# A fused MLP on one core: the first token chunk loaded and turned in two halves, with a new order of the first matmuls

## The chip, the cores and the metric

The kernel runs on one core of one Trainium2 chip. The metric is the device time of one execution in microseconds. Before the change the median of five runs is 93.78 us (93.72 to 94.08).

## The reference

The kernel computes a two-layer perceptron with a tanh-approximated GELU on 2048 tokens, 448 features and 1792 hidden units, all in bf16:

```
B, S, D, F = 1, 2048, 448, 1792
h = jnp.einsum("bsd,df->bsf", x, w1) + b1
h = jax.nn.gelu(h, approximate=True)
return jnp.einsum("bsf,fd->bsd", h, w2) + b2
```

## The kernel before

**Tiling.** The tokens are worked in four chunks of 512 (SC = 512, HC = 256). A chunk runs layer 1 completely, and then layer 2. Layer 1 puts hidden units on the 128 partitions and 512 tokens on the free axis: 14 F-tiles of 128 hidden units, taken as 7 pairs. The 448 features are contracted as three full slices of 128 (k = 0, 1, 2) and a remainder of 64 (k = 3). Layer 2 puts tokens on the partitions and contracts the 14 F-tiles.

**Two half-arrays.** Every contraction of 128 rows is split into two of 64 rows, one on each half of the TensorE array, so matmuls come in twos that run side by side on two PSUM banks. Of an F-tile pair, part "a" gives tile 0 the lower rows and tile 1 the upper ones, and part "b" the other way round. Part "a" has the slices k = 0 to 2; part "b" has these and the remainder. For the remainder the rows of w1 are in w1r: loaded on the upper 64 partitions, and copied for the odd tiles to the lower ones by VectorE (L399, event w1rU). In this text a "step" is one such couple of matmuls for one k; L0.a(0,256) means part a of pair 0 on the first 256 tokens, three half-wide steps.

**PSUM.** There are four units of two banks; units go round: pair 0 has u0, pair 1 u1, pair 2 u2, pair 3 u3, pair 4 u0 again. A pair may start when the two GELU activations that read its unit's former content are done. ScalarE does one activation of 128x512 for each F-tile (L269), with the bias b1.

**The start.** Chunks 1 to 3 of x are turned by DMA transposes. Chunk 0 is loaded as it stands (xn, L153) with four consecutive tokens on each partition, and TensorE turns it by 64-row transposes against an identity (L344): for every half h of 256 tokens and every slice k, one block of four transposes, and four for the remainder rows out of xr, which VectorE has collected from xn (L362). Copies out of PSUM into xT follow, on VectorE and ScalarE (L357 for the slices, L384 for the remainder). Until x is there, TensorE runs 7 dependence-free matmuls of 512 columns and one of 256 (warm, L192).

**Queues.** Loads come from two hardware queues. The queue of SyncE (SPq, DMA queue q1) issues x, then waits until ScalarE has loaded its table (an activation on a constant), and then issues w1r's first part, w1's third part (F-tiles 4 to 7), w1r's second part, w1's fourth part (tiles 8 to 13), w2 in two parts, b2, and the transposes. The queue of ScalarE (ACTq, DMA queue q10) issues w1's first two parts: ("w1", 0) with F-tiles 0 and 1, ("w1", 1) with tiles 2 and 3. b1 comes over GpSimd's queue, and VectorE turns it (four 32x32 transposes, L181, and a cast, L183) after the copy of w1r's first part and before that of its second.

**The order of the work** is written out by hand: each engine executes its list in order, and each instruction waits for the events that it names. On TensorE at the start the list is: warm; the first half's blocks; L0.a(0,256); the last block and the remainder's; L1.a(0,256); L0.a(256,512); L1.a(256,512); L0.b; L1.b; L2.a; and from there L3.a, L2.b, L4.a, L3.b and so on, all 512 wide. The two blocks of the second half for k = 0 and 1 go with the first half's, ahead of L0.a.

Of the kernel before, what the change touches and what calls it, by code (L numbers as in the profile page):

```python
# [7 lines left out]
BF16 = mybir.dt.bfloat16  # L8
# [65 lines left out]
def bass_standalone__dense_activation_gelu__prompt_kernel(  # L74
# [8 lines left out]
    B, S, D = x.shape  # L83
    F = w1.shape[1]
    P = 128
    H = P // 2
    SC = 512
    HC = SC // 2
    assert B == 1 and S % SC == 0 and F == 14 * P and D == 3 * P + H
    x2, out2 = x[0], out[0]  # L90
    NSC, NST, STC, NFT = S // SC, S // P, SC // P, F // P
    NPAIR = NFT // 2
    KT = 3
    D3 = KT * P
    DH = D // 2
    NWARM = 7

    with ExitStack() as es:
        sb = lambda name, shape, dt: es.enter_context(nc.sbuf_tensor(name, shape, dt))
        xn = sb("xn", [P, STC, D], BF16)  # L100
        xr = sb("xr", [P, STC // 2, P], BF16)
        ident = sb("ident", [P, P], BF16)
        xT = sb("xT", [P, KT + 1, S], BF16)
# [10 lines left out]
        out_sb = sb("out_sb", [P, NST, D], BF16)  # L114
        unit = [es.enter_context(nc.psum_tensor(f"u{i}", [P, 2, SC], FP32)) for i in range(4)]

        pr = Program(nc, es)
# [10 lines left out]
        def load_w1(i, engine="sync"):  # L128
            c0, c1 = W1CUTS[i] * P, W1CUTS[i + 1] * P
            pr.dma(engine, lambda e: e.dma_start(  # L130
                w1_sb[:, :, c0:c1], w1[0:D3, c0:c1].rearrange("(k p) f -> p k f", p=P)), ("w1", i))
# [3 lines left out]
        def load_w1r(i, engine="sync"):  # L135
            cs = slice(RCUTS[i] * P, RCUTS[i + 1] * P)
            pr.dma(engine, lambda e: e.dma_start(w1r[H:P, cs], w1[D3:D, cs]), ("w1r", i))

        def load_w2(a, b):
            pr.dma("sync", lambda e: e.dma_start(  # L140
                w2_sb[:, a:b, :], w2[a * P:b * P, :].rearrange("(f p) d -> p f d", p=P)), ("w2", a))
# [6 lines left out]
                xT[:, slot, s0:s1], x2[s0:s1, d0:d0 + P], transpose=True), event, after)  # L148


        x0v = x2[0:SC, :].rearrange("(p t) d -> p t d", t=STC)
        o0v = out2[0:SC, :].rearrange("(p t) d -> p t d", t=STC)
        pr.dma("sync", lambda e: e.dma_start(xn[:, :, :], x0v), "x")  # L153
        pr.barrier("sync", ["table"])
        load_w1r(0)
        load_w1(2)
        load_w1r(1)
        load_w1(3)
        load_w2(0, 7)
# [2 lines left out]
        for c in range(1, NSC):  # L162
            for slot in range(KT + 1):
# [5 lines left out]
            out=ident[:, :], in_=ident[:, :], compare_op=ALU.not_equal, fill=1.0,  # L169
# [4 lines left out]
               after=["b1z"])  # L174
        pr.op("scalar", lambda e: e.activation(junk[:, :], one, ACT.Gelu_apprx_tanh), event="table")  # L175
        load_w1(0, "scalar")
        load_w1(1, "scalar")

        def turn_b1():
            for q in range(4):  # L180
                pr.op("vector", lambda e, q=q: e.transpose(  # L181
                    b1t[32 * q:32 * q + 32, :], b1n[:, 32 * q:32 * q + 32]), after=["b1n"], event=("b1t", q))
            pr.op("vector", lambda e: e.tensor_copy(b1_f[:, :], b1t[:, 0:NFT]),  # L183
                  after=[("b1t", q) for q in range(4)], event="b1")
# [5 lines left out]
        def warm(n, cols=SC):  # L190
            for _ in range(n):
                pr.op("tensor", lambda e: e.matmul(unit[0][:, 0, 0:cols], lhsT=ones_w, rhs=ones_m[:, 0:cols],  # L192
                                                   start=True, stop=True))
# [3 lines left out]
        busy = {}  # L197
# [24 lines left out]
        class Layer1:  # L222
# [33 lines left out]
                for k in range(KT):  # L256
                    self.step("a", k, t0, t1)

            def b(self, t0=0, t1=SC):
                for k in range(KT + 1):  # L260
                    self.step("b", k, t0, t1)
                if t1 == SC:
                    self.act()

            def act(self):
                c, u = self.c, self.u
# [5 lines left out]
                    busy[(u, lo)] = ("g", c, ft)  # L272

        def store(j, after):
            pr.dma("sync", lambda e: e.dma_start(o0v[:, j, :] if j < STC else out2[j * P:(j + 1) * P, :], out_sb[:, j, :]), "out", after=after)

        class Layer2:

# [58 lines left out]
        def spot(u, i, rows=slice(0, P)):  # L337

            return unit[u][rows, :, i * H:(i + 1) * H].bitcast(BF16).rearrange("p b (t s) -> p b t s", t=2)

        def turn(o, i, event, after):

            for half, rows in enumerate(HALVES):
                pr.op("tensor", lambda e, half=half, rows=rows: e.transpose(o(half), i(rows), ident[rows, rows]),  # L344
                      after=["ident"] + after, event=event if half else None)

        def turn_block(h, k, u, i, wait=()):
            for t in (0, 1):
                turn(lambda half, t=t: spot(u, i)[:, half, t, :], lambda rows, t=t: xn[rows, 2 * h + t, k * P:(k + 1) * P],
                     ("xt", h, k) if t else None, ["x"] + list(wait))  # L350

        def drain_blocks(engine, h, ks, u, wait=None):
            n = len(ks)
            o = xT[:, ks[0]:ks[0] + n, h * HC:(h + 1) * HC].rearrange("p k (t b s) -> p k b t s", b=2, t=2)
            f = unit[u][:, :, 0:n * H].bitcast(BF16).rearrange("p b (k t s) -> p k b t s", k=n, t=2)
            for i in range(n):
                pr.op(engine, lambda e, i=i: (e.copy if engine == "scalar" else e.tensor_copy)(o[:, i], f[:, i]),  # L357
                      after=[wait or ("xt", h, ks[-1])], event=("xT0", h, ks[i]))
            busy[(u, 0)] = ("xT0", h, ks[-1])

        def turn_first():
            pr.op("vector", lambda e: e.tensor_copy(  # L362
                xr[:, :, :].rearrange("p q (two h) -> p q two h", two=2),
                xn[:, :, D3:D].rearrange("p (q two) h -> p q two h", two=2)), after=["x"], event="xr_in")
            for k, engine in enumerate(("vector", "scalar", "vector")):
                turn_block(0, k, k, 0)
                drain_blocks(engine, 0, (k,), k)
            turn_block(1, 0, 3, 0)
            turn_block(1, 1, 3, 1)
            drain_blocks("scalar", 1, (0, 1), 3)  # L370

        def turn_rest():


            turn_block(1, 2, 2, 0, [("xT0", 0, 2)])
            for q in range(STC // 2):
                turn(lambda half, q=q: spot(2, 1)[:, half, q, :], lambda rows, q=q: xr[rows, q, :], ("xr", q), ["xr_in"])
            drain_blocks("vector", 1, (2,), 2, ("xr", 1))
            for src, engine in enumerate(("vector", "scalar")):
                i = spot(2, 1, HALVES[src])  # L380
                for dst in (src, 1 - src):
                    o = xT[HALVES[dst], KT, 0:SC].rearrange("p (q two b s) -> p b q two s", q=2, two=2, b=2)[:, :, :, src, :]
                    pr.op(engine, lambda e, o=o, i=i, engine=engine:
                          e.copy(o, i) if engine == "scalar" else e.tensor_copy(o, i),  # L384
                          after=[("xr", 1), ("xT0", 1, 2)], event=("xR0", dst, src))
            busy[(2, 1)] = ("xR0", 1, 0)
            busy[(2, 2)] = ("xR0", 0, 1)

        warm(NWARM)
        warm(1, HC)  # L390
        turn_first()
        L = [Layer1(0, j) for j in range(NPAIR)]
        L[0].a(0, HC)
        turn_rest()

        for i in (0, 1):
            odd = lambda rows, i=i: w1r[rows, RCUTS[i] * P:RCUTS[i + 1] * P].rearrange(
# [2 lines left out]
                  after=[("w1r", i)], event=("w1rU", i))  # L400
            if i == 0:
                turn_b1()
        L[1].a(0, HC)
        L[0].a(HC, SC)
        L[1].a(HC, SC)
        L[0].b()
        L[1].b()
        L[2].a()
        for j in range(3, NPAIR):
            L[j].a()  # L410
            L[j - 1].b()
        L[-1].b()

        for c in range(NSC):
# [7 lines left out]
            else:  # L422

                pr.op("vector", lambda e: e.tensor_copy(b2_z[H:H + 1, :], b2_bc[H:H + 1, :]),  # L424
                      after=["b2", "b2z0"], event="b2z")
# [3 lines left out]
            p = Layer2(c, (0, 1))  # L429
            if c + 1 < NSC:  # L430
                q = Layer2(c, (2, 3))
# [5 lines left out]
            else:  # L437
                q, r = Layer2(c, (2,)), Layer2(c, (3,), True)
# [37 lines left out]
```

## Time and profile before

| | us |
|---|---|
| median of five runs | 93.78 |
| the profiled execution, whole | 93.8 |
| its span, first to last instruction | 92.5 |
| TensorE busy in the span | 89.2 |
| ScalarE busy | 38.4 |
| VectorE busy | 13.5 |
| first matmul of the warm-up | 0.78 |
| first transpose of x | 4.17 |
| first matmul of layer 1 | 4.93 |
| second group of layer 1 (pair 1) | 5.56 |

A busy time is the sum over the time in which the engine had at least one instruction in work. The difference of 1.3 us between the execution and its span lies ahead of the first and behind the last instruction. Times of single instructions below are counted from the start of the span. In a line of the timeline the columns are: start, length, engine, source line, operation, what it writes and reads, and how many instructions were merged; in brackets, idle time of that engine ahead of it and what ended it.

### The profile page before, as it was taken

To read this page: it belongs to the slowest core of one execution; us is meant where nothing else is said; L and a number is where in the kernel's file an instruction comes from. 1 tells how busy PE (TensorE), PEld (TensorE's weight loads), DVE (VectorE), ACT (ScalarE), POOL (GpSimd) and SP (SyncE) were. 2 spreads that over 40 slices of the span, in tenths; PEclk is the share of its full clock that TensorE was granted. 3 is DMA by queue.
4 is the path that set the end of the run, shared out by engine and by line. 5 is a ranking of instruction groups with operands and counts; after the bars stand their busy time and mean duration, and the time that the engine had idled before them with its cause. 6 is when DMAs were issued, how large, how long until landed. Compare 5 with 4: busy or idle time off the path is not lost.

```text
span 92.5 us, 2086 instructions
## 1 busy us (share of the span) xinstructions
PE 89.2 (96%) x945; PEld 45.8 (50%) x945; DVE 13.5 (15%) x34; ACT 38.4 (42%) x64; POOL 1.7 (2%) x8
## 2 busy tenths in 40 slices
PE   6989999999999999999999999999999999999990
PEld 2374444555544444555554444555554444475890
DVE  0165001100441000000432000000333000000421
ACT  6064978600005788700003787900002888900001
POOL 6000000000000000000000000000000000000000
PEclk9999999999999999999999999999999999999999
DMA  2999999549247000000033000000022000000022
GB/s 48 330 290 328 380 323 135 118 99 109 56 96 216 4 7 0 0 0 0 0 105 101 0 4 0 7 0 0 0 99 99 7 0 0 0 0 7 27 72 99
DMA packets 12744, 7.32 MB, mean 79 GB/s; under 512 B 6976, under 2 KB 12544, under 8 KB 12736
## 3 DMA queue, kind: packets, MB, share of 16 engines
q1 hardware_dynamic: 11904, 6.80, 29.6%
q10 hardware_dynamic: 800, 0.39, 1.4%
q8 instruction: 7, 0.11, 0.5%
q14 instruction: 1, 0.01, 0.0%
q0 software_dynamic: 32, 0.00, 0.0%
HBM read 3.79 MB, written 1.84 MB: 61 GB/s over the span
## 4 chain that ended last, share of the span: by engine, by line
PE 96%; DVE 1%; issue 0%
PE u L217 92%; PE u L192 4%; PE u L344 0%; DVE out_sb L326 0%; DVE xT L357 0%
## 5 line engine op out<-in xcount | busy, mean ns | idle before, releaser
L269 ACT ACTIVATE g<-u,b_f 128x512 bf16<-128x512 f32 x56 | 34.9, 686 | 39.4 <-PE u L217 38.0
L217 PE MATMUL u<-w_sb,g 64*128 64x448 bf16 (+1 forms) x504 | 43.2, 328 | 0.0
L217 PE MATMUL u<-xT,w_sb 64*128 64x512 bf16 (+1 forms) x348 | 41.0, 369 | 0.2 <-DVE xT L357 0.2
L217 PEld LDWEIGHTS u<-w_sb,g 64*128 64x128 bf16 x504 | 24.5, 94 | 18.4
L217 PEld LDWEIGHTS u<-xT,w_sb 64*128 64x128 bf16 x348 | 16.8, 94 | 19.4 <-DMA w_sb<-in_w_dram 0.3
L312 DVE TENSOR_TENSOR out_sb<-u,b_bc 128x448 bf16<-128x448 f32 x14 | 8.1, 620 | 60.7 <-PE u L217 60.7
L217 PE MATMUL u<-xT,w1r 64*128 64x512 bf16 x56 | 10.6, 376 | 0.0
L217 PEld LDWEIGHTS u<-xT,w1r 64*128 64x128 bf16 x56 | 2.7, 94 | 3.3
L329 ACT CAST out_sb<-u 128x224 bf16<-128x224 f32 x1 | 0.3, 346 | 9.2 <-PE u L217 9.2
L192 PE MATMUL u<-const-bfloat16-1.0 128*128 128x512 bf16 (+1 forms) x8 | 3.4, 601 | 0.8 <-PEq L461 0.8
L192 PEld LDWEIGHTS u<-const-bfloat16-1.0 128*128 128x128 bf16 x8 | 1.0, 139 | 2.4 <-issue 2.4
L357 ACT COPY xT<-u 128x256 bf16<-128x256 bf16 x3 | 0.9, 380 | 2.3 <-PE u L344 2.3
L175 ACT ACT_TABLE_LOAD x1 | 1.3, 1283 | 0.7 <-PEq L461 0.7
L424 DVE COPY b_z<-b_bc 1x448 bf16<-1x448 bf16 x1 | 0.3, 267 | 6.8 <-DMA b_bc<-in_b_dram 6.8
L187 DVE COPY xT<-xT 64x512 bf16<-64x512 bf16 x3 | 0.9, 289 | 2.2 <-DMA xT<-in_x_dram 2.1
L344 PEld LDWEIGHTS u<-ident,xn 64*128 64x128 bf16 x24 | 0.7, 102 | 0.7 <-issue 0.7
L384 ACT COPY xT<-u 64x256 bf16<-64x256 bf16 x2 | 0.7, 368 | 0.5 <-DVE xT L357 0.5
L357 DVE COPY xT<-u 128x256 bf16<-128x256 bf16 x3 | 0.8, 287 | 0.8 <-PE u L344 0.8
L320 DVE TENSOR_TENSOR out_sb<-u,b_bc 128x448 bf16<-128x448 f32 x1 | 0.6, 625 | 1.7 <-PE u L217 1.7
L181 DVE STREAM_TRANSPOSE b1t<-b1n 32x32 bf16<-32x32 bf16 x4 | 0.8, 202 | 0.1
L344 PE MATMUL u<-ident,xn 64*128 64x64 bf16 x24 | 0.8, 199 | 0.0
L362 DVE COPY xr<-xn 128x256 bf16<-128x256 bf16 x1 | 0.2, 226 | 3.1 <-DMA xn<-in_x_dram 3.1
(18 smaller groups left out, 4.8 us busy)
## 6 DMA issues: line engine op xcount, KB each, us to landing
out_dram<-out_sb SPq DMA_DIRECT2D x16, 112.0 KB, 1.7
w_sb<-in_w_dram SPq DMA_DIRECT2D x2, 784.0 KB, 8.0
w_sb<-in_w_dram SPq DMA_DIRECT2D x1, 576.0 KB, 5.7
xn<-in_x_dram SPq DMA_DIRECT2D x1, 448.0 KB, 3.3
w_sb<-in_w_dram ACTq DMA_DIRECT2D x2, 192.0 KB, 4.1
w_sb<-in_w_dram SPq DMA_DIRECT2D x1, 384.0 KB, 4.6
xT<-in_x_dram SPq DMA_TRANSPOSE x12, 3.5
w1r<-in_w_dram SPq DMA_DIRECT2D x1, 160.0 KB, 4.4
```

The lines of the kernel that those rows point to most:

```text
L175: pr.op("scalar", lambda e: e.activation(junk[:, :], one, ACT.Gelu_apprx_tanh), event="table")
L181: pr.op("vector", lambda e, q=q: e.transpose(b1t[32 * q:32 * q + 32, :], b1n[:, 32 * q:32 * q + 32]), after=["b1n"], event=("b1t", q))
L187: pr.op("vector", lambda e: e.tensor_copy(xT[0:H, KT, s0:s1], xT[H:P, KT, s0:s1]), after=after, event=event)
L192: pr.op("tensor", lambda e: e.matmul(unit[0][:, 0, 0:cols], lhsT=ones_w, rhs=ones_m[:, 0:cols], start=True, stop=True))
L217: o = pr.op("tensor", lambda e: e.matmul(unit[u][:, lo, cols], lhsT=lhsT, rhs=rhs, start=start, stop=stop, skip_group_check=skip), after=a ...
L269: pr.op("scalar", lambda e, lo=lo, ft=ft: e.activation(g[:, ft, c * SC:(c + 1) * SC], unit[u][:, lo, :], ACT.Gelu_apprx_tanh, bias=b1_f[:, ...
L312: pr.op("vector", lambda e, lo=lo, j=j: e.tensor_tensor(out=out_sb[:, j, :], in0=unit[u][:, lo, 0:D], in1=b2_bc[:, :], op=ALU.add), after= ...
L320: pr.op("vector", lambda e: e.tensor_tensor(out=out_sb[:, j, :].rearrange("p (two h) -> p two h", two=2), in0=unit[u][:, :, 0:DH], in1=b2_ ...
L329: pr.op("scalar", lambda e: e.copy(out_sb[:, j, DH:D], unit[u][:, 1, 0:DH]), after=[y[1]], event=("o", j, 1))
L344: pr.op("tensor", lambda e, half=half, rows=rows: e.transpose(o(half), i(rows), ident[rows, rows]), after=["ident"] + after, event=event i ...
L357: pr.op(engine, lambda e, i=i: (e.copy if engine == "scalar" else e.tensor_copy)(o[:, i], f[:, i]), after=[wait or ("xt", h, ks[-1])], eve ...
L384: e.copy(o, i) if engine == "scalar" else e.tensor_copy(o, i),
```

## The change

x of chunk 0 is loaded by two DMAs of 256 tokens each, with two consecutive tokens on a partition. The first is issued on SyncE's queue, the second on ScalarE's behind w1's first part; w1's second part goes over to SyncE's queue, behind the first half of x and ahead of the wait for the table. w1's third part now comes ahead of w1r's first. There is one full warm-up matmul fewer. The first half of x is turned alone (turn_0), and L0.a, L1.a and the slices of L0.b run on it; then the second half is turned (turn_1: blocks k = 0, 2, 1 and the remainder), and the rest of pairs 0 and 1 follows in half-wide steps. The remainder steps of pairs 0 and 1 (b_last), with their activations, come after L2.a. All three copies of the second half wait for transposes of turn_1; before, two of them followed on the first half's blocks. Where xn's rows lie in the output changes with the load, so the stores of chunk 0 are indexed by halves.

```diff
-    NWARM = 7
+    NWARM = 6
...
-        x0v = x2[0:SC, :].rearrange("(p t) d -> p t d", t=STC)
-        o0v = out2[0:SC, :].rearrange("(p t) d -> p t d", t=STC)
-        pr.dma("sync", lambda e: e.dma_start(xn[:, :, :], x0v), "x")
+        def load_x(h, engine):
+            pr.dma(engine, lambda e: e.dma_start(
+                xn[:, 2 * h:2 * h + 2, :], x2[h * HC:(h + 1) * HC, :].rearrange("(p t) d -> p t d", t=2)), ("x", h))
+
+        o0v = [out2[h * HC:(h + 1) * HC, :].rearrange("(p t) d -> p t d", t=2) for h in (0, 1)]
+        load_x(0, "sync")
+        load_w1(1)
         pr.barrier("sync", ["table"])
+        load_w1(2)
         load_w1r(0)
-        load_w1(2)
         load_w1r(1)
         load_w1(3)
...
         load_w1(0, "scalar")
-        load_w1(1, "scalar")
+        load_x(1, "scalar")
...
-            def b(self, t0=0, t1=SC):
-                for k in range(KT + 1):
+            def b_main(self, t0=0, t1=SC):
+                for k in range(KT):
                     self.step("b", k, t0, t1)
-                if t1 == SC:
-                    self.act()
+
+            def b_last(self):
+                self.step("b", KT)
+                self.act()
...
+        def drain_block(engine, h, k, u, i, after):
+            o = xT[:, k, h * HC:(h + 1) * HC].rearrange("p (t b s) -> p b t s", b=2, t=2)
+            f = spot(u, i)
+            pr.op(engine, lambda e: (e.copy if engine == "scalar" else e.tensor_copy)(o, f),
+                  after=after, event=("xT0", h, k))
+            busy[(u, int(engine == "scalar"))] = ("xT0", h, k)
+
+        def turn_0():
+            for k, engine in enumerate(("vector", "scalar", "vector")):
+                turn_block(0, k, k, 0)
+                drain_block(engine, 0, k, k, 0, [("xt", 0, k)])
+
+        def turn_1():
             pr.op("vector", lambda e: e.tensor_copy(
                 xr[:, :, :].rearrange("p q (two h) -> p q two h", two=2),
-                xn[:, :, D3:D].rearrange("p (q two) h -> p q two h", two=2)), after=["x"], event="xr_in")
-            for k, engine in enumerate(("vector", "scalar", "vector")):
-                turn_block(0, k, k, 0)
-                drain_blocks(engine, 0, (k,), k)
+                xn[:, :, D3:D].rearrange("p (q two) h -> p q two h", two=2)), after=[("x", 0), ("x", 1)], event="xr_in")
             turn_block(1, 0, 3, 0)
-            turn_block(1, 1, 3, 1)
-            drain_blocks("scalar", 1, (0, 1), 3)
-        def turn_rest():
-            turn_block(1, 2, 2, 0, [("xT0", 0, 2)])
+            turn_block(1, 2, 3, 1)
+            turn_block(1, 1, 2, 0, [("xT0", 0, 2)])
             for q in range(STC // 2):
                 turn(lambda half, q=q: spot(2, 1)[:, half, q, :], lambda rows, q=q: xr[rows, q, :], ("xr", q), ["xr_in"])
-            drain_blocks("vector", 1, (2,), 2, ("xr", 1))
+            drain_block("vector", 1, 0, 3, 0, [("xt", 1, 2)])
+            drain_block("scalar", 1, 1, 2, 0, [("xr", 1)])
+            drain_block("vector", 1, 2, 3, 1, [("xt", 1, 2)])
...
-        turn_first()
+        turn_0()
         L = [Layer1(0, j) for j in range(NPAIR)]
         L[0].a(0, HC)
-        turn_rest()
+        L[1].a(0, HC)
+        L[0].b_main(0, HC)
+        turn_1()
...
-        L[1].a(0, HC)
-        L[0].a(HC, SC)
-        L[1].a(HC, SC)
-        L[0].b()
-        L[1].b()
+        L[1].b_main(0, HC)
+        for j in (0, 1):
+            L[j].b_main(HC, SC)
+        for j in (0, 1):
+            L[j].a(HC, SC)
         L[2].a()
+        for j in (0, 1):
+            L[j].b_last()
```

More of the change, by code (lines that the diff above doesn't have):

```diff
@@ L257, in a, with b @@
                     self.step("a", k, t0, t1)
-            def b(self, t0=0, t1=SC):
-                for k in range(KT + 1):
+            def b_main(self, t0=0, t1=SC):
+                for k in range(KT):
                     self.step("b", k, t0, t1)
-                if t1 == SC:
-                    self.act()
+            def b_last(self):
+                self.step("b", KT)
+                self.act()
+            def b(self):
+                self.b_main()
+                self.b_last()
             def act(self):
@@ L274, in store @@
         def store(j, after):
-            pr.dma("sync", lambda e: e.dma_start(o0v[:, j, :] if j < STC else out2[j * P:(j + 1) * P, :], out_sb[:, j, :]), "out", after=after)
+            pr.dma("sync", lambda e: e.dma_start(o0v[j // 2][:, j % 2, :] if j < STC else out2[j * P:(j + 1) * P, :], out_sb[:, j, :]), "out", after=after)
         class Layer2:
@@ L349, in turn_block @@
                 turn(lambda half, t=t: spot(u, i)[:, half, t, :], lambda rows, t=t: xn[rows, 2 * h + t, k * P:(k + 1) * P],
[L350 to L359, printed above, removed]
@@ L361, in turn_first @@
-        def turn_first():
+                     ("xt", h, k) if t else None, [("x", h)] + list(wait))
+        def drain_block(engine, h, k, u, i, after):
[8 more added lines that the diff above has]
+                drain_block(engine, 0, k, k, 0, [("xt", 0, k)])
@@ L384, in turn_rest @@
                           e.copy(o, i) if engine == "scalar" else e.tensor_copy(o, i),
-                          after=[("xr", 1), ("xT0", 1, 2)], event=("xR0", dst, src))
+                          after=[("xr", 1), ("xT0", 1, 1)], event=("xR0", dst, src))
             busy[(2, 1)] = ("xR0", 1, 0)
```

## The prediction

> **What bounds the kernel now.** I began with the page: its first line and its chain of work by engine.
>
> ```profile
> span 92.5 us, 2086 instructions
> ...
> PE 96%; DVE 1%; issue 0%
> ```
>
> TensorE carries the whole chain. Only idle or slow TensorE time can be won, so I took the chain next, piece by piece (start, length, what, how many).
>
> ```profile
> 0.78 3.36 PE u L192 x8
> 4.14 0.02 issue
> 4.17 0.30 PE u L344 x4
> 4.47 0.02 issue
> 4.49 0.30 DVE xT L357
> 4.79 0.14 issue
> 4.93 0.50 PE u L217 x6
> 5.43 0.12 PE u L344 x8
> 5.55 0.01 issue
> 5.56 84.75 PE u L217 x903
> 90.31 0.38 DVE out_sb L326
> ```
>
> From 5.56 to 90.31 matmuls stand back to back; an edit that takes none of them away moves the end only by moving that dense stretch. Up to 5.56 the chain is warm-up, transposes, one copy, and L0.a(0,256). What released L1.a at 5.56? It needs w1's second part. The answer on w1's DMAs of ScalarE's queue:
>
> ```profile
> L130 ACTq DMA_DIRECT2D w_sb<-in_w_dram x2: 446/478/511, 0.8 to 1.3; - x2
> ...
> DMA to landing us min/median/max: 3.9/4.1/4.2
> ```
>
> Issued at 0.80 and 1.28 (timeline), they land at 0.80 + 3.9 = 4.7 and 1.28 + 4.2 = 5.5. The load of x lands at 0.75 + 3.3 = 4.05. So a landing, not arithmetic, opens the dense stretch. Then the order in which the queues were served: the DMA answer for 1.7 to 3.2 us, and for 3.65 to 4.3.
>
> ```profile
> q1 hardware_dynamic: 113, 0.40, 88.3%
> ```
>
> ```profile
> q10 hardware_dynamic: 455, 0.22, 115.4%
> ```
>
> First x alone (q1), then both parts of w1 alone (q10), although x and w1's first part were issued within 0.05 us. Last, VectorE's timeline, because "remainder rows late" touches what hangs on it, and the line of the waits that shows it binding:
>
> ```profile
> 6.57 0.22 DVE L399 COPY w1r<-w1r 64x256 bf16<-64x256 bf16 x1
> 6.82 0.90 DVE L181 STREAM_TRANSPOSE b1t<-b1n 32x32 bf16<-32x32 bf16 x4
> 7.86 0.17 DVE L183 CAST b_f<-b1t 128x14 f32<-128x14 bf16 x1
> ```
>
> ```profile
> ACT g L269 <- DVE b_f L183: 1.4, 1, 1.4
> ```
>
> The first activation (8.13) waits for the bias, which waits for the copy of w1r: 8.13 - 6.57 = 1.56 us from that copy's start to the activation.
>
> **What the Trainium skill says.** "DMA: Bandwidth & Descriptors", section "Issuing engines are not separate DMA queues": loads from several queues run on the same 16 DMA engines, so a second queue brings no bandwidth. The trace agrees (the two windows above). The same page, "Queues, rings and completion order": an engine round-robins between queues by packets. Here it served whole loads in turn; I saw no finer mixing. "TensorE: Matmul & The Clock Gate", Part 1: TensorE runs at half clock until a window of about 3.4 us was busy; Part 4 of it says that transposes don't count as busy. The trace agrees on the first: warm-up matmuls of 512 columns start every 0.43 us, later couples of 512 every 0.216 (remainder couples at 7.20 and 8.06 with three others between). Of the first half's transposes 8 start from 4.17 to 4.33 and 12 in the next 0.17 us, so the clock rose near 4.33, 3.55 us after the first matmul. On the second no run here says anything.
>
> **The change part by part.**
>
> *First half of x.* x is 0.46 MB; q1 moved 0.40 MB in 1.5 us at 88%, so 0.30 MB/us, and half of x is 0.75 us less ahead of everything behind it. It lands at about 4.05 - 0.75 = 3.3.
>
> *Warm-up.* One matmul less is 0.43 us: the half-wide last one starts at 3.72 - 0.43 = 3.29 and holds the array 0.21 us, to about 3.51. The first transpose goes from 4.17 to 3.54; x's first half is there, so the warm-up sets this.
>
> *First copies.* Transpose to copy 0.32 (4.17 to 4.49), copy 0.30, copy to matmul 0.14; cold transposes add 0.03: L0.a at 3.54 + 0.79 = 4.33, before 4.93. w1's first part lands at 4.7 - 0.75 = 3.95, hidden.
>
> *Work ahead of the second half.* A half-wide step is 0.109 us (9 steps from 5.56 to 6.55). L0.a ends at 4.66. w1's second part, now third in the line, lands at 5.5 - 0.75 = 4.75; its own issue at about 1.15 on SyncE's queue sits in time in which that queue waited for the table. L1.a starts at about 4.79, and six steps (0.65) end at 5.44.
>
> *Second half of x.* It is the last of the same 0.85 MB that landed by 5.5 before. x landed about 0.4 us after its last packets (by 3.65), w1's second part 0.7 after its own (by 4.8): bounds 5.2 and 5.5. I take 5.25, since its descriptors are x's kind. VectorE's xr copy (0.23) ends at about 5.5.
>
> *Turning it.* 16 transposes at some 15 ns, 5.44 to 5.68; the last four start behind the xr copy. Before, two of the second half's blocks and their copies went under the wait for w1; now all of them are on the path, and what covers their copies is L1.b_main(0,256), 0.33 us, to 6.00. VectorE's first copy starts 0.25 after its transposes (5.36 to 5.61 before), 5.79, ends 6.08: first step of L0.b_main(256,512) at 6.13. ScalarE's copy waits for the last transpose (5.66 + 0.23), takes 0.38, ends 6.27: second step at 6.33. VectorE's other copy ends about 6.29, in time. So 0.23 us of stall. From 6.33, 11 half-wide steps take 1.20: L2.a could start at 7.53. Before, L2.a started at 8.28 with two remainder steps (0.43) done that now come later; like for like 7.85. Gain 0.32 us. Twelve full steps in twenty-four half-wide ones cost 24 x 0.109 - 12 x 0.216, under 0.03 us.
>
> *w1's third part* landed at 2.87 + 4.6 = 7.5; with w1r's 64 KB behind it, 0.2 us sooner, 7.3: hidden, with 0.2 to spare. ScalarE's remainder copies (0.76 from 6.27) free u2 at about 7.05, hidden.
>
> *w1r late.* Its first part now lands where both ended before, between 7.0 and 7.5; I take 7.2. Behind that wait on VectorE stand the turn of b1 and so all activations: the first at 7.2 + 0.02 + 1.56 = 8.78. The two of pair 0 end 1.27 later (the pair lengths of 1.26 and 1.27 in ScalarE's timeline), 10.05, and L4.a, which needs u0, could start at 10.10. TensorE reaches L4.a at 7.53 + 0.65 + 0.43 + 0.65 + 0.86 = 10.12 (before, 10.43). So there is no stall, by 0.02 us; later pairs have 1.51 us on TensorE against 1.27 on ScalarE, so it isn't repeated. If w1r lands at 7.5 it is 0.28 us.
>
> *Stores* of chunk 0 move the same rows of 896 bytes: nothing, hidden under layer 1 of the next chunk.
>
> Sum: a gain of 0.32 (the half-wide steps are in it). The span goes from 92.5 to 92.2; the profiled execution, 93.8 with 1.3 outside its span, is that of the median 93.78: about 93.46.
>
> **The rivals.**
>
> *A, as worked out:* 93.46, by itself 93.3 to 93.55 (second half of x at 5.2 to 5.35). Chance 0.54.
>
> *B, the bias wait takes the gain:* w1r lands at 7.5, L4.a waits until 10.4, and all of the earlier start is idle there: 93.46 + 0.28 = 93.74. For it: a straggling landing of w1's third part at 7.5, whose place w1r inherits. Against: its load is small. 0.13.
>
> *C, the second half of x lands no earlier than w1's second part did (5.5), or the two queues' loads mix and w1's first part lands late:* start of the dense part gains 0.1: 93.65 to 93.75. 0.11.
>
> *D, slower, the clock:* the warm-up ends at 3.51 and TensorE then has only transposes and a pause until 4.33. If that window no longer counts as busy, the clock rises one window later (3.4 us). Cold work costs half its time, up to 1.7 us, less some 0.3 of stalls that it fills: 93.46 + 1.4 = 94.9. It turns faster into slower once more than (0.32 + 0.28) x 2, 1.2 us, of cold work is added, so a clock rising after about 5.6. Against: the window from 0.9 to 4.3 keeps 2.6 of 3.4 us of plain matmuls. 0.12.
>
> *E, slower by landings:* w1r or w1's third part beyond 7.85: 94.0 to 94.3. 0.10.
>
> **How the numbers follow.** The likeliest is A: 93.46. 0.3% is 0.28 us, about what a measurement of this kernel tells from no change, so 93.50 divides faster from same. Faster: 0.46 of A's 0.54. Same: the other 0.08 of A, and B and C, 0.32. Slower: D and E, 0.22. The range 93.2 to 94.3 leaves out D and a little beyond A.
>
> **What would show it.** First transpose near 3.54 and L0.a near 4.33 in the chain; the second half's landing near 5.25; a stall of some 0.2 us ahead of L0.b_main(256,512); L2.a near 7.53; first activation near 8.8 behind L183; L4.a near 10.15. Wrong it would be if couples after 4.33 are still 0.2 us apart for 256 columns (D), if L4.a waits long for ScalarE (B, E), or if w1's first part lands after 4.4 (C).

## The result: slower by 0.69%, and what the profile after shows

The changed kernel takes 1.0069 times as long as the kernel before (95% interval 1.0055 to 1.0084). The profiled execution takes 94.6 us with a span of 93.3, before 93.8 and 92.5. Twelve of the changed kernel's 43 executions took 95.5 to 96.9 us, as none of the 80 of the kernel before did; the ratio leaves these out, as every ratio below leaves out its like, and where the profiled execution of an experiment was such a one (e2 and e10), only landings and the pace of the first matmuls are read from it.

The chain of work that ended last, of the changed kernel, in order of time (start, length, what; the pieces ahead of 2.27, up to the end of the wait for the table, are left out):

```profile
2.27 0.38 SPq L130
2.64 0.04 issue
2.69 5.54 DMA w1r<-in_w_dram
8.22 0.02 issue
8.25 0.22 DVE w1r L410
...
9.54 0.19 DVE b_f L187
...
9.81 1.27 ACT g L279 x2
11.09 0.14 issue
11.22 79.89 PE u L221 x849
91.11 0.38 DVE out_sb L336
```

Before, the chain ran along TensorE from the warm-up to the end. Now it comes to TensorE only at 11.22, at L4.a, by way of ScalarE's activations of pair 0, the cast of b1, the copy of w1r's rows, and the load of w1r. TensorE's dense stretch then ends at 91.11 instead of 90.31. So all of the loss, 0.80 us, has been made by L4.a. In the timeline of the kernel before, L2.a started at 8.28 and L4.a at 10.43:

```profile
8.28 2.11 PE L217 MATMUL u<-xT,w_sb 64*128 64x512 bf16 x18
10.43 1.46 PE L217 MATMUL u<-xT,w_sb 64*128 64x512 bf16 x12
```

Where it was made stands in TensorE's timeline of the changed kernel from 3.7 us on. A line can merge matmuls of two widths: of the 36 that start at 6.24, 30 are half-wide, and the last 6, from 8.11, are L2.a.

```profile
3.71 0.35 PE L354 MATMUL u<-ident,xn 64*128 64x64 bf16 x12
4.42 0.50 PE L221 MATMUL u<-xT,w_sb 64*128 64x256 bf16 x6 [0.36 <-DVE xT L365]
5.34 0.83 PE L221 MATMUL u<-xT,w_sb 64*128 64x256 bf16 x12 [0.42 <-DMA w_sb<-in_w_dram]
6.00 0.34 PE L354 MATMUL u<-ident,xn 64*128 64x64 bf16 x12
6.18 0.22 PE L354 MATMUL u<-ident,xr 64*128 64x64 bf16 x4
6.24 2.68 PE L221 MATMUL u<-xT,w_sb 64*128 64x256 bf16 x36
8.76 0.59 PE L221 MATMUL u<-xT,w1r 64*128 64x512 bf16 x4
9.19 1.46 PE L221 MATMUL u<-xT,w_sb 64*128 64x512 bf16 x12
10.48 0.38 PE L221 MATMUL u<-xT,w1r 64*128 64x512 bf16 x2
11.22 1.47 PE L221 MATMUL u<-xT,w_sb 64*128 64x512 bf16 x12 [0.36 <-ACT g L279]
```

Two losses can be read off. First, L2.a starts three full steps of 0.216 ahead of the remainder steps at 8.76, at 8.11; like for like, without the two remainder steps that now come later, it would have started at 7.84 before: 0.27 us late. Second, the remainder step of pair 2 starts at 10.48 and L4.a would follow at 10.70; it starts at 11.22, released by ScalarE: 0.52 us. Together 0.79.

The first is made up of two things. L1.a starts at 5.34, only 0.22 us earlier than before (5.56), because it waits for w1's second part. And behind that start now stand 0.23 us of transposes (6.00 to 6.24) and 0.24 us of stall on their copies, where before the transposes were over when L1.a started and no such stall followed: 0.47 less 0.22 is 0.25 of the 0.27.

First the wait at 5.34. The first line of the next answer is w1's first part, the second its second part; the last line gives the time from issue to landing, so that 1.2 + 4.1 = 5.3.

```profile
L130 ACTq DMA_DIRECT2D w_sb<-in_w_dram x1: 435/435/435, 0.8 to 0.8; - x1
L130 SPq DMA_DIRECT2D w_sb<-in_w_dram x1: 419/419/419, 1.2 to 1.2; - x1
...
DMA to landing us min/median/max: 3.5/3.8/4.1
```

The halves of x land at 0.75 + 2.8 = 3.55 and 1.27 + 4.2 = 5.5. And from 3.7 to 4.7 us both queues moved loads at the same time, w1's second part (q1) and the second half of x (q10):

```profile
q10 hardware_dynamic: 125, 0.20, 55.9%
q1 hardware_dynamic: 321, 0.16, 53.4%
```

What comes first in the queues is slow already, as shows in what q1 moved of x from 1.7 to 2.7 us. Before the change:

```profile
q1 hardware_dynamic: 59, 0.21, 84.2%
```

and after it:

```profile
q1 hardware_dynamic: 77, 0.14, 81.9%
```

The DMA engines were as busy, but with rows of half the size they moved two thirds of the bytes.

The second loss is seen in VectorE's timeline of the changed kernel:

```profile
8.25 0.22 DVE L410 COPY w1r<-w1r 64x256 bf16<-64x256 bf16 x1 [0.70 <-DMA w1r<-in_w_dram]
8.50 0.90 DVE L185 STREAM_TRANSPOSE b1t<-b1n 32x32 bf16<-32x32 bf16 x4
9.54 0.17 DVE L187 CAST b_f<-b1t 128x14 f32<-128x14 bf16 x1
```

From the copy of w1r to the first activation it is 9.81 - 8.25 = 1.56 us, as before; only the copy, which started at 6.57, now waits for a landing at 8.2. The activations, ready at TensorE from about 9.2, wait for the bias.

### The profile page after: what moved, and what is told of

Read it like the earlier page. It is cut to its first block, busy times and chain, and to the rows that moved or that the text cites. A ratio compares the mean times of both kernels' runs of the same rounds, so it can differ in the third digit from the quotient of the medians.

```text
span 93.3 us, 2111 instructions
## 1 busy us (share of the span) xinstructions
PE 89.1 (96%) x956; PEld 51.7 (55%) x956; DVE 13.7 (15%) x35; ACT 37.9 (41%) x63; POOL 1.7 (2%) x8
## 3 DMA queue, kind: packets, MB, share of 16 engines
HBM read 3.79 MB, written 1.84 MB: 60 GB/s over the span
## 4 chain that ended last, share of the span: by engine, by line
PE 86%; DMA 6%; ACT 2%; DVE 2%; issue 1%; ACTq 1%; SPq 0%; DVEq 0%
PE u L221 86%; DMA w1r<-in_w_dram 6%; ACT g L279 1%; DVE b1t L185 1%; ACTq L152 1%; ACT L179 1%; DVE out_sb L336 0%; SPq L130 0%; DVE w1r L410 0%; ACT junk L179 0%; DVE b_f L187 0%; DVEq L63 0%; ACTq L63 0%
## 5 line engine op out<-in xcount | busy, mean ns | idle before, releaser
L221 PE MATMUL u<-xT,w_sb 64*128 64x512 bf16 (+1 forms) x360 | 41.7, 362 | 1.1 <-DMA w_sb<-in_w_dram 0.4
L221 PEld LDWEIGHTS u<-w_sb,g 64*128 64x128 bf16 x504 | 27.7, 94 | 15.3
L221 PEld LDWEIGHTS u<-xT,w_sb 64*128 64x128 bf16 x360 | 19.5, 94 | 18.1 <-DMA w_sb<-in_w_dram 1.1
L196 PE MATMUL u<-const-bfloat16-1.0 128*128 128x512 bf16 (+1 forms) x7 | 2.9, 594 | 0.8 <-PEq L474 0.8
L410 DVE COPY w1r<-w1r 64x256 bf16<-64x256 bf16 (+1 forms) x2 | 0.6, 288 | 0.7 <-DMA w1r<-in_w_dram 0.7
```

What stands on the lines that cost most here:

```text
L221: o = pr.op("tensor", lambda e: e.matmul(unit[u][:, lo, cols], lhsT=lhsT, rhs=rhs, start=start, stop=stop, skip_group_check=skip), after=a ...
```

## The experiments

Two theories were set against others. Theory 1: the larger loss is the bias, which is queued on VectorE behind w1r's late landing. Theory 2: the rest comes from the late second part of w1 with the work behind it, that is, from the loads. The rivals: the new order of the work itself, the shorter warm-up, the pauses of TensorE. Times are ratios to the kernel before, with 95% intervals. The edits are against the changed kernel unless another base is named; "..." stands for lines that are not shown.

### e1: the bias freed of w1r

```diff
-            pr.op("vector", lambda e, odd=odd: e.tensor_copy(odd(slice(0, H)), odd(slice(H, P))),
+            if i == 0:
+                pr.op("scalar", lambda e, odd=odd: e.copy(odd(slice(0, H)), odd(slice(H, P))),
+                      after=[("w1r", i)], event=("w1rU", i))
+            else:
...
```

> The changed kernel, with w1r's first copy (to the lower partitions) on ScalarE, so that on VectorE the turn of b1 no longer stands behind the landing of w1r. Theory 1 (the bias wait is the larger loss): the first activation starts near 9.2 us behind TensorE's remainder step of pair 0 and not near 9.8 behind the bias cast, L4.a needn't wait for ScalarE and starts near 10.7 instead of 11.22, and the time falls by 0.4 to 0.6 us from the changed kernel, to a ratio of 1.001 to 1.003 against the kernel before. Rival (the late second half of x and late w1 bound the start by themselves, the bias wait only fills their time): the ratio stays at 1.005 to 1.008.

Measured: 1.0019 (1.0002 to 1.0036), clear of the changed kernel's interval. In the timeline of e1, VectorE, and then ScalarE:

```profile
7.69 0.90 DVE L185 STREAM_TRANSPOSE b1t<-b1n 32x32 bf16<-32x32 bf16 x4
8.72 0.18 DVE L187 CAST b_f<-b1t 128x14 f32<-128x14 bf16 x1
```

```profile
8.10 0.40 ACT L411 COPY w1r<-w1r 64x256 bf16<-64x256 bf16 x1 [0.35 <-DMA w1r<-in_w_dram]
9.29 1.84 ACT L279 ACTIVATE g<-u,b_f 128x512 bf16<-128x512 f32 x3 [0.79 <-DVE w1r L414]
```

w1r lands at 8.1, late as in the changed kernel, but the bias is there at 8.9 and the first activation starts at 9.29, with TensorE's first remainder step begun at 8.88. L4.a starts at 10.82 right behind pair 2. That is theory 1's 0.5 us (0.0050 of some 94). What the chain of e1 then rests on:

```profile
1.20 4.21 DMA w_sb<-in_w_dram
5.41 0.05 issue
5.46 0.83 PE u L221 x12
6.29 0.23 PE u L354 x16
6.52 84.17 PE u L221 x903
```

It is w1's second part, with TensorE carrying the rest: the chain of the remaining loss begins where theory 2 has it.

### e2: w1r ahead of w1's third part again

```diff
-        load_w1(2)
         load_w1r(0)
+        load_w1(2)
```

> The changed kernel with w1r's first part ahead of w1's third part again, as before the change. Theory 1: w1r lands some 0.5 to 1 us sooner, the bias is ready near 9.1, the wait of L4.a goes, and what is left is a later w1 third part, 0 to 0.2 us of wait at L2.a: ratio 1.001 to 1.004. Rival (a straggling DMA engine holds whichever load comes there): w1r lands near 8 all the same, ratio 1.005 to 1.008.

Measured: 1.0043 (1.0012 to 1.0073), from five of nine executions. w1r's first part landed 4.3 us after its issue at 2.27, at 6.6 instead of 8.2, so no straggler held whatever came there. The interval covers what theory 1 and its rival expected of the time; the landing speaks for the order of the loads, the time decides nothing.

### e3: the new order of the work with the old loads

```diff
-    NWARM = 6
+    NWARM = 7
...
-        load_x(0, "sync")
-        load_w1(1)
+        pr.dma("sync", lambda e: e.dma_start(xn[:, :, :], x0v), "x")
         pr.barrier("sync", ["table"])
-        load_w1(2)
         load_w1r(0)
+        load_w1(2)
...
-        load_x(1, "scalar")
+        load_w1(1, "scalar")
...
```

> The order of the work of the changed kernel, with the loads of the kernel before: x in one DMA, w1's first two parts on ScalarE's queue, w1r ahead of w1's third part, seven full warm-up matmuls. Theory 2 (the new order of the work needs the early half; with x whole it pays for the transposes of the second half and their copies on the path): L2.a starts near 8.3 against 8.12 in the changed kernel, no bias wait, L4.a near 10.9: ratio 1.004 to 1.006. Rival (the loads are what the change spoils, the order of work itself costs nothing): ratio 0.999 to 1.002.

Measured: 1.0044 (1.0028 to 1.0059). This kernel, with the old loads, loses 0.4 us: the loads are not all of it. It agrees with theory 2's reading that the order of the work pays for transposes and copies on the path and needs a half of x that comes early. The profiled execution had L2.a at 8.83, not 8.3; its 18 matmuls of 256 columns from 4.87 to 6.71 took 1.84 us where 18 in the kernel before took 0.99, so its clock was low until then. How much of the 0.4 us is the order and how much a later clock is therefore not told apart.

### e5: the warm-up as before

```diff
-    NWARM = 6
+    NWARM = 7
```

> The changed kernel with seven full warm-up matmuls as before. First transpose at 3.94 instead of 3.71. Theory 1 (landings set the start of the dense stretch): nothing, ratio 1.006 to 1.008 as for the changed kernel. Rival (the shorter warm-up leaves TensorE's clock low for longer): ratio 1.003 or less.

Measured: 1.0073 (1.0047 to 1.0099), from six executions. The longer warm-up gives nothing back, and the rival of the shorter warm-up, which asked for 1.003 or less, falls as the cause of the 0.69%. The clock itself this doesn't settle: e5's own profile shows it low for long, as the last section has it.

### e6: the second half of x behind w1's second part

On the base of e1:

```diff
         load_w1(1)
+        load_x(1, "sync")
         pr.barrier("sync", ["table"])
...
-        load_x(1, "scalar")
```

> The kernel with w1r's copy on ScalarE (bias wait gone), and the second half of x issued on SyncE's queue behind w1's second part instead of on ScalarE's, so that it can't be served ahead of or among it. Theory 2a (the two queues' loads mix, and w1's second part pays for it): that part lands near 5.0 instead of 5.4, L1.a starts near 5.05, L2.a near 7.9 to 8.0 instead of 8.24, time down by 0.2 to 0.3 us, ratio 0.999 to 1.000. Rival (the half loads are slow in themselves, mixing costs nothing): w1's second part still lands at 5.3 to 5.4, ratio 1.001 to 1.003.

Measured: 1.0037 (1.0015 to 1.0059). The loads did as theory 2a says: w1's second part landed 3.7 us after its issue at 1.2, at 4.9, and there was no pause ahead of L1.a:

```profile
4.58 1.21 PE L221 MATMUL u<-xT,w_sb 64*128 64x256 bf16 x18 [0.26 <-DVE xT L365]
5.63 0.34 PE L354 MATMUL u<-ident,xn 64*128 64x64 bf16 x12
```

In the six profiles that keep the changed kernel's first loads (its own and e1, e2, e5, e7 and e8) it landed at 5.3 to 5.9. So mixing did delay that part, by some 0.4 us or more. But the time isn't better than e1's, and the 0.999 to 1.000 of theory 2a did not come. In this profile L4.a waited at the end for w1's fourth part, at 10.52, and so the lead of 0.4 us was cut to 0.3; over all executions not even that is seen. Why the mean doesn't follow the profile stays open.

### e7: L0.b ahead of L1.a

On the base of e1:

```diff
-        L[1].a(0, HC)
         L[0].b_main(0, HC)
+        L[1].a(0, HC)
         turn_1()
```

> The kernel with w1r's copy on ScalarE, and L0.b_main(0,256) ahead of L1.a(0,256) on TensorE: it needs only w1's first part, so it can fill the wait for the second. Theory 2 (what sets the dense stretch is w1's second part with the work queued behind it): TensorE is at the second half of x near 5.75 instead of 6.13, L2.a near 7.9, ratio 0.998 to 1.000. Rival (the second half of x and its copies set it): no change, ratio 1.001 to 1.003.

Measured: 1.0026 (1.0005 to 1.0047): no gain, and the figure of the rival, that the second half of x and its copies set the start. In the profile L0.b filled the pause, and then L1.a still waited, since w1's second part landed only at 5.9 in that execution:

```profile
4.53 1.15 PE L221 MATMUL u<-xT,w_sb 64*128 64x256 bf16 x12 [0.26 <-DVE xT L365]
5.91 0.50 PE L221 MATMUL u<-xT,w_sb 64*128 64x256 bf16 x6 [0.22 <-DMA w_sb<-in_w_dram]
```

The same wait in another place. That this load is late agrees with theory 2. But of the 0.2 to 0.3 us that e1 leaves, neither e6 nor e7 got anything back, so what part of them the loads have is not shown.

### e8: the pauses filled

```diff
         turn_0()
+        warm(1, SC, 3)
         L = [Layer1(0, j) for j in range(NPAIR)]
         L[0].a(0, HC)
+        warm(1, SC, 3)
         L[1].a(0, HC)
...
```

> The changed kernel with one warm-up matmul of 512 columns more in each of TensorE's two pauses (after the first half's transposes and after L0.a), into PSUM that isn't in use yet. Theory 3 (the pauses let TensorE's clock rise later): the couples of 256 columns are 0.109 us apart from 4.4 on, ratio down to 1.003 to 1.005. Rival (landings alone): the ratio stays at 1.006 to 1.008.

Measured: 1.0062 (1.0035 to 1.0089). The middle is the rival's figure, but the interval also takes in most of what theory 3 gave (1.003 to 1.005), so a part for the clock isn't excluded.

### e9 and e11: a try at a better kernel

Both halves of x on SyncE's queue, w1's first two parts on ScalarE's, w1r ahead of w1's third part; turn_1 right after L0.a; remainder steps ahead of L2.a. e11 adds one warm-up matmul after turn_0.

```diff
         load_x(0, "sync")
-        load_w1(1)
+        load_x(1, "sync")
         pr.barrier("sync", ["table"])
-        load_w1(2)
         load_w1r(0)
+        load_w1(2)
...
-        load_x(1, "scalar")
+        load_w1(1, "scalar")
...
         L[0].a(0, HC)
-        L[1].a(0, HC)
-        L[0].b_main(0, HC)
         turn_1()
...
-        L[1].b_main(0, HC)
-        for j in (0, 1):
-            L[j].b_main(HC, SC)
-        for j in (0, 1):
-            L[j].a(HC, SC)
-        L[2].a()
+        L[0].b_main(0, HC)
+        L[1].a(0, HC)
+        L[0].b_main(HC, SC)
+        L[1].a(HC, SC)
+        L[0].a(HC, SC)
+        L[1].b_main()
         for j in (0, 1):
             L[j].b_last()
+        L[2].a()
```

> A try at a kernel better than both: halves of x both on SyncE's queue, w1's first two parts on ScalarE's, w1r ahead of w1's third part; turn_1 right after L0.a(0,256), then L0.b_main(0,256), L1.a(0,256) and the rest, remainder steps ahead of L2.a. If the half of x pays once w1's second part is needed later: dense from near 5.2, L2.a near 7.9 to 8.0 (with the remainder steps done; before 8.28), ratio 0.996 to 0.998. If the second half's copies or w1's third part bind: ratio 0.999 to 1.003.

> The kernel of both ideas (halves of x on SyncE's queue, turn_1 after L0.a, remainder steps ahead of L2.a) with one warm-up matmul of 512 columns in the pause after the first half's transposes. If the pause lets the clock rise later: 93.5 to 93.8 for most, ratio 0.996 to 0.998. If not: 0.998 to 1.000 as without it.

Measured: e9 0.9989 (0.9968 to 1.0010), e11 0.9999 (0.9980 to 1.0017). With the early half of x used where only w1's first part is needed, and the remainder not moved, the whole loss is gone; a gain on the kernel before isn't shown. Several things change together here, and which of them took the loss away isn't told apart. The profile of e9 says why not more: TensorE has no wait for a load, but its first steps ran at half the pace. TensorE's timeline of e9:

```profile
4.43 0.82 PE L221 MATMUL u<-xT,w_sb 64*128 64x256 bf16 x6 [0.26 <-DVE xT L365]
```

Six matmuls of 256 columns take 0.82 us, where the changed kernel's at 4.42 take 0.50 and start their successors sooner. The filler of e11 didn't change it: there the same six take 0.82 from 4.71.

### e10: only the size of the rows

The kernel before; x in one DMA, but with rows of 1792 bytes.

```diff
-        x0v = x2[0:SC, :].rearrange("(p t) d -> p t d", t=STC)
+        x0v = x2[0:SC, :].rearrange("(h p t) d -> p h t d", h=2, t=2)
...
```

> The kernel before, with one edit: x's first chunk still comes in one DMA, but with rows of 1792 bytes instead of 3584 (two tokens on a partition for each half, as in the change). Theory 4 (the first packets are bound by their number, not by their bytes, so halving the rows loses what halving the load was to win): x lands 0.2 to 0.5 us later than 4.05, w1's first two parts as much later, ratio 1.002 to 1.005. Rival (bytes count): x lands at 4.0 to 4.1, ratio 0.999 to 1.001.

Measured: 1.0026 (1.0005 to 1.0046), from 12 of 22 executions. x landed after 3.7 us instead of 3.3, and from 1.7 to 2.7 us q1 moved this:

```profile
q1 hardware_dynamic: 85, 0.15, 72.2%
```

0.15 MB in 85 packets, against 0.21 in 59 with the full rows. So in this microsecond a packet of half the size took more than half the time: worked out from the shares of 16 engines, an estimate, 0.23 us of an engine for a packet of the full rows (0.842 x 16 / 59), 0.17 for one of the changed kernel's and 0.14 for one here. It is neither bytes alone nor, as theory 4 has it, packets alone. Half rows cost 0.4 us of landing and a quarter of a percent of the time with no other change to the loads or the order of the work; the landing and the time are theory 4's.

### e12 and e13: the remainder part alone

The kernel before, with w1r behind w1's third part and the remainder steps of pairs 0 and 1 behind L2.a (e12); and with the copy of w1r on ScalarE in addition (e13).

```diff
-        load_w1r(0)
         load_w1(2)
+        load_w1r(0)
...
-        L[0].b()
-        L[1].b()
+        L[0].b_main()
+        L[1].b_main()
         L[2].a()
+        L[0].b_last()
+        L[1].b_last()
```

> The kernel before, with only the remainder part of the change: w1r's first part behind w1's third, and the remainder steps of pairs 0 and 1 behind L2.a. Theory 1a (rows late costs only because all loads have become later as well): w1r lands near 7.5, the first activation near 9.1, L4.a waits 0 to 0.1 us, ratio 0.999 to 1.002. Rival (rows late costs its half microsecond by itself): L4.a waits 0.4 us or more, ratio 1.004 to 1.006.

> The kernel before with the remainder part of the change alone, and in addition w1r's first copy on ScalarE, so that the bias doesn't stand behind w1r. If the bias wait is what rows late cost by themselves: ratio 0.999 to 1.001, against 1.0027 without this copy. If it is w1's fourth part, which L4.a waited for in the profile of the remainder part alone: ratio 1.002 to 1.004 again, and L4.a released by that load.

Measured: e12 1.0027 (1.0009 to 1.0044), e13 1.0019 (1.0000 to 1.0038). The remainder part costs something by itself, less than the half microsecond in the changed kernel. Which wait it is there the two don't tell apart. In e12's profile L4.a waited for w1's fourth part, which landed 7.2 us after its issue at 3.94 (5.7 before):

```profile
10.17 0.38 PE L217 MATMUL u<-xT,w1r 64*128 64x512 bf16 x2
11.20 0.39 PE L217 MATMUL u<-xT,w_sb 64*128 64x512 bf16 x2 [0.65 <-DMA w_sb<-in_w_dram]
```

and in e13's it landed at 10.0 and TensorE went on to L4.a at 10.29 without a wait. The bias was late in e12 as well. Its VectorE:

```profile
7.70 0.22 DVE L405 COPY w1r<-w1r 64x256 bf16<-64x256 bf16 x1 [1.07 <-DMA w1r<-in_w_dram]
```

From there the first activation follows at 9.26, and with 1.27 for the pair and 0.14 to the matmul the bias alone would have held L4.a until about 10.67, an estimate, where pair 2 let go of TensorE at 10.39.

## Why the prediction was wrong

It said 93.46 us and faster; the kernel is slower by 0.69%. The likeliest case fell. What came is rival E, with part of C: w1r and w1's third part beyond 7.85, to which the prediction gave one chance in ten, and a loss larger than E's 94.0 to 94.3. L4.a was forecast for 10.12 and came at 11.22. Of these 1.10 us 0.58 were there at L2.a (8.11 for 7.53), and 0.52 are the wait for ScalarE. The steps that failed are three landings: the first half of x, w1's second part, and w1r, the last with the bias behind it.

- **What bounds the kernel** was right: landings open the dense stretch, and an edit that moves them moves the end. The end moved by just what L4.a moved, 0.8 us.
- **First half of x** failed. This step took 0.30 MB/us from x as a whole and turned half the bytes into 0.75 us. Half of x landed at 3.55, not 3.3, so 0.5 us sooner (in other profiles with this load 3.3 to 3.8): rows of half the size move fewer bytes in the first microsecond (0.14 MB against 0.21), as e10 showed by itself. w1's first part, worked out with the same 0.75, landed at 0.8 + 3.5 = 4.3, not at 3.95.
- **Warm-up and first copies** were nearly right: transposes at 3.71 for 3.54, L0.a at 4.42 for 4.33. The first transpose comes 0.16 us after x's landing here, and in e1 and e6, where x landed at 3.64, at 3.78 and 3.82; so the landing of x seems to set it, not the warm-up.
- **Work ahead of the second half** failed by the largest single step at the start: w1's second part landed at 5.3 and not at 4.75. The later first half of x has a part in that, but not the larger: in e8 the first half landed at 3.34, as forecast, and w1's second part at 5.3 all the same. The rest is the mixing of the two queues (e6, which put both loads on one queue, had this one at 4.9). The prediction set mixing aside because it had seen whole loads served in turn. That reading was wrong already of the kernel before: it holds for x ahead of w1's parts up to 3.2 us and for 3.65 to 4.3, but from 4.3 to 4.8 both queues moved loads at once there too:

```profile
q10 hardware_dynamic: 198, 0.09, 63.2%
q1 hardware_dynamic: 71, 0.06, 61.1%
```

With x's second half and w1's second part waiting on two queues they are served together, as "DMA: Bandwidth & Descriptors" of the Trainium skill, section "Queues, rings and completion order", says of queues with work; the windows from 3.7 to 4.7 us of the changed kernel, 55.9% and 53.4%, agree.
- **Second half of x** landed at 5.5, the late bound of 5.2 to 5.5. It didn't bind: TensorE came to it at 6.0.
- **Turning it** was right in its size: between 6.24 and L2.a the prediction counted 0.23 us of stall, and from 6.24 to 8.11 there are 15 steps of 0.109 (1.64) and 0.24 of stall. What it missed is that the start of L1.a, 0.77 us earlier in its sum, was to pay for these and came only 0.22 earlier.
- **w1r late** had the mechanism whole and the size wrong. The 1.56 us from the copy to the first activation is exact. The landing was taken at 7.2, because w1r would inherit the place in which w1's third part landed before (7.5 with its straggler); it landed at 8.2. So L4.a was held 0.52 us instead of not at all, and e1 got 0.5 us back by taking the bias from behind this wait. The step had an edge of 0.02 us between stall and none, on a landing whose bounds were 0.5 us apart; it should have been the likeliest loss, not a tie. In e12 and e13, with the same order of w1r and w1's third part but the first loads of the kernel before, w1r landed at 7.7 and 7.5. So 0.3 to 0.5 of the 1.0 us that the landing was off belongs to its place in the queue, and the rest came with the new first loads. From 6.2 to 7.2 us the queue moved 0.19 MB, where the microsecond before it had moved 0.37; before the change it was 0.25 and 0.36. What slows it there was not tried.
- **Rival D**, the clock, is not what the two compared profiles show: in the changed kernel's the six matmuls of L0.a stand as close as before. But it is not ruled out. The mark that the prediction named, couples of 256 columns 0.2 us apart, is in other profiles: up to 6.5 us in e3 and 6.6 in e5, and beyond 9 us in e2 (96.23 us) and e10 (96.14). The same 36 matmuls that the changed kernel does in 2.68 us from 6.24 take 3.62 in e2, which differs from it only in the order of two later loads; the same 24 take 1.80 in the kernel before and 3.42 in e10:

```profile
7.48 3.62 PE L221 MATMUL u<-xT,w_sb 64*128 64x256 bf16 x36
```

```profile
5.56 1.80 PE L217 MATMUL u<-xT,w_sb 64*128 64x256 bf16 x24
```

```profile
6.19 3.42 PE L217 MATMUL u<-xT,w_sb 64*128 64x256 bf16 x24
```

These 0.9 and 1.6 us are of the size that D gave (1.4). None of the 12 executions of e8, whose pauses are filled, took over 95.1 us. Whether the fillers did that, and whether the pauses or the later landing of x bring the late clock, no run decides.

## What to carry to other kernels

A load in two halves wasn't half as late here: its rows were half as long, and the first microsecond moved two thirds of the bytes. So look at the first microsecond of the queue before crediting half the bytes. Work that comes onto the path with the halves has to be paid by the earlier start; here 0.47 us of it met 0.22. When a load is put later, follow what its waiter holds up in its own engine's list; here a bias that had landed at 5.7 (1.83 + 3.9) was not turned before 8.5, behind a copy that it had nothing to do with. And where a step is safe by less than the spread of the landing that it rests on, count it as a loss.

## What the runs showed that was not expected

TensorE's clock rises at different times in different executions of nearly the same start. In the kernel before it rose near 4.33. In e5, with the same warm-up, 18 matmuls of 256 columns stood like this, where the kernel before did 18 in 0.99 us:

```profile
4.84 2.14 PE L221 MATMUL u<-xT,w_sb 64*128 64x256 bf16 x18 [0.26 <-DVE xT L365]
6.82 0.34 PE L354 MATMUL u<-ident,xn 64*128 64x64 bf16 x12
```

In the 2 us to the first transpose only some 0.15 us is a wait, ahead of L1.a; the rest is pace, nine couples 0.213 us apart. "TensorE: Matmul & The Clock Gate" of the Trainium skill, Part 1, says that the window is free-running and isn't reset when a kernel starts; the runs agree, with a clock that rose near 4.33 in one execution and after 6.6 in another behind the same warm-up. So one profile of a kernel with such a start can be half a microsecond and more off its like, and only many executions told the kernels apart.
